# Attention scores as split products on two row halves of TensorE, two tiles at a time

## The chip, the core and the metric

The kernel runs on one core of a Trainium2 chip. Its metric is the device time in microseconds (us) of one execution. The engines named here are TensorE (PE, with its weight loads as PEld), VectorE (DVE), ScalarE (ACT), GpSimd (POOL), and the queue of SyncE (SP), which issues the DMAs.

## The reference, cut to what matters

```python
# q, k, v: (8, 12, 448, 64) float32; g_q, g_k: (64,)
q_n, k_n = rmsnorm(q, g_q), rmsnorm(k, g_k)            # over the last axis
scores = (1 / 8) * q_n @ k_n^T                         # 448 x 448 for each of 96 heads
attn = softmax(scores)                                 # with the row maximum taken off
x = (attn @ v) as (3584, 768)
h = x @ w_in; g = h * cos(h); out = g @ w_out          # w_in 768 x 2048, w_out 2048 x 768
```

All of it is float32. The scores, the part that changes, are 96 products of 448 queries by 448 keys over 64 dimensions.

## The kernel before

The 96 heads are worked on as 48 pairs of two heads; the two heads' 64 dimensions lie on partitions 0 to 63 and 64 to 127. Six pairs make one batch. The 896 query rows of a pair are cut into seven tiles of 128 rows: tiles 0 to 2 are of the first head, 4 to 6 of the second, and tile 3 holds the last 64 rows of the first and the first 64 of the second (its unused quarters are zeros in the queries). Each tile's scores are a PSUM bank of 128 x 448; three banks `S` take turns. VectorE scales a bank and takes its row extremes (`rowmin`, L572), ScalarE makes the exponentials into SBUF (`expo`, L580), TensorE turns them (`transp`, L614 to L623), ScalarE and VectorE split the turned ones into a high and a low part (`pt_high` L637, `pt_low` L644), and TensorE multiplies them by the values (`av`, L661 and L663). The feed-forward product of the batch before runs between (`ffn1`, L745 to L747, `ph`). When the last pair is done, a second stage does the rest of the feed-forward part (L819 to L821).

The first six pairs multiply in plain float32: `score_plain` (L552) takes the 64 rows of one head for tiles 0 to 2 and 4 to 6, two tiles (j and j + 4) one after the other in the program, and all 128 rows for tile 3. A plain float32 matmul of 448 columns shows as two records. `av_plain` (L679, L683, L689) is the plain product with the values, with 64 columns of weights.

From the seventh pair on (42 pairs) a float32 number is split into two numbers of the faster type float32r, x = hi + lo, and a product is qhi khi + qlo khi + qhi klo. `k_high`, `k_low`, `q_high`, `q_low` make the four parts. For tile 3, `score` (L554 to L568) multiplies these three products over all 128 rows. For the six other tiles it needs two matmuls, since 64 dimensions of a head fill half of the rows: the rows of `kboth` (tile `M`) hold khi on partitions 0 to 63 and klo on 64 to 127, those of `qtwo` (tile `D`) hold qhi twice, and those of `qlow` (tile `E`) hold qlo above zeros. DMAs bring the parts to these places: `d_place`, `e_place` and `m_place`, seven transfers a pair.

The order of the work on each engine is made before the kernel is built. `Plan` (L24 to L165) takes every step with its engine, a cost, a due time and the buffers that it reads and writes, and runs the five engines against each other by these costs; the order in which steps start there is the order in which they are emitted. Steps are added by `prepare` (L944), `attend` (L1004) and `multiply`. `SHIFT` moves due times; `RING` holds the number of buffers. TensorE gets a step's matmuls as one unbroken run.

Of the kernel before, what the change touches and what calls it, by code (L numbers as in the profile page):

```python
# [10 lines left out]
F32 = mybir.dt.float32  # L11
# [12 lines left out]
class Plan:  # L24
# [7 lines left out]
        "st_load": 7.0, "m_place": 6.5, "d_place": 6.5, "e_place": 6.5, "v_load": 5.5, "v_fetch": 7.0, "w_load": 7.0,  # L32
# [4 lines left out]
    TWICE = ("rk_spread", "rs_load", "d_place", "m_place")  # L37
# [131 lines left out]
def tile_attention_moe(  # L169
# [11 lines left out]
    nc = tc.nc  # L181
# [36 lines left out]
    gs = cpool.tile([128, 6], F32, tag="gs", name="gs")  # L218
    gsc = {False: gs[:, 5:6], True: gs[:, 4:5]}
# [5 lines left out]
    def g_load():  # L225
        nc.sync.dma_start(gs[:, 0:4], gg)

    def g_fold():
        nc.vector.scalar_tensor_tensor(
            gs[:, 4:6], gs[:, 0:2], -float(D) / math.sqrt(D), gs[:, 2:4], op0=ALU.mult, op1=ALU.mult  # L230
        )
# [107 lines left out]
    def keep(name, n):  # L339
        return [apool.tile([128, n], F32R, tag=f"{name}{i}", name=f"{name}{i}", bufs=1) for i in range(2)]  # L340

    qtwo = keep("D", 768)
    kplain = [apool.tile([128, 2 * S], F32, tag=f"M{i}", name=f"kn{i}", bufs=1) for i in range(2)]
    kplain += [apool.tile([128, 2 * S], F32, tag="lo", name=f"km{i}", bufs=RING["lo"]) for i in range(2)]
    kplain.append(apool.tile([128, 768], F32, tag="E1", name="km4", bufs=1))
    KHOME = (0, 1, 2, 3, 4, 2)
    kboth, qlow = {}, [apool.tile([128, 768], F32R, tag="E0", name="E0", bufs=1)]
# [17 lines left out]

    def e_clear(i):
        if i:
            qlow.append(apool.tile([128, 768], F32R, tag="E1", name="E1", bufs=1))
        nc.vector.tensor_scalar(
            qlow[i][64:128], ident[64:128, 0:1].broadcast_to([64, 768]), 0.0, 0.0, op0=ALU.mult, op1=ALU.add  # L370
        )
# [30 lines left out]
    def km(u):  # L402
        return kplain[KHOME[u]][:, :512]
# [50 lines left out]
    def rkb(u):  # L454
        return (qtwo[u % 2][:, :S] if u < NP else kboth[u % 2][:, S:]).bitcast(F32)

    def rk_spread(u):
        spread(rkb(u), rk_d[u].rearrange("p t -> (p t)"))

    def rk_load(u):  # L460
        if u < NP + 2:
            kboth[u % 2] = apool.tile([128, 2 * S], F32R, tag=f"M{u % 2}", name=f"M{u % 2}", bufs=1)
        row = rk_d[u].rearrange("p t -> (p t)").rearrange("(o h s) -> o h s", o=1, h=2)
        nc.sync.dma_start(rkb(u), row.broadcast_to([64, 2, S]))
# [7 lines left out]
    def k_norm(u):  # L472
        if u >= NP:
            nc.gpsimd.tensor_tensor(kd, kd, rkb(u), ALU.mult)
            return
        for a, c, n in ((0, 64, 0), (64, 0, 384)):
            nc.gpsimd.tensor_tensor(km(u)[a:, c : c + S - n], kd[a:, n:], rkb(u)[a:, n:], ALU.mult)

    def k_high(u):
        nc.scalar.copy(tl(u, "khi", [128, S], F32R), kd)  # L480

    def k_low(u):
        nc.gpsimd.tensor_tensor(tl(u, "kl", [128, S], F32R), kd, pair[u]["khi"].bitcast(F32), ALU.subtract)
# [16 lines left out]

    def m_place(u, low):
        src = pair[u]["kl" if low else "khi"].bitcast(F32)
        dst = kboth[u % 2].bitcast(F32)[64 * low : 64 * low + 64]
        nc.sync.dma_start(dst[:, 384:512], src[:, 384:])
        dst = bass.AP(dst.tensor, dst.offset, [dst.ap[0], [512, 2], [1, 384]])
        nc.sync.dma_start(dst, src[:, :384])

    def d_place(u):
        for a in (0, 64):
            nc.sync.dma_start(qtwo[u % 2].bitcast(F32)[a : a + 64], pair[u]["qhi"].bitcast(F32)[:, :384])  # L510

    def e_place(u):
        nc.sync.dma_start(qlow[u % 2].bitcast(F32)[:64], pair[u]["ql"].bitcast(F32)[:, :384])
# [322 lines left out]
    def y_store(b, oc, src):  # L836
# [19 lines left out]
    def add(eng, cost, due, fn, *args, **more):  # L856
        name, first = fn.__name__, args[0] if args else 0
        stage = 0
        if name in ("ffn1", "h_out", "h_store", "h_both", "x_split"):
            stage = int(first < (NP if name == "x_split" else 1))  # L860
        elif name[:2] not in ("w_", "v_", "e_") or name in ("v_load", "v_high", "v_low", "v_plain", "e_place"):
# [12 lines left out]
        cost *= {DVE: 1.059, ACT: 1.026, POOL: 1.021}.get(eng, 1.0)  # L874
        plan.add(eng, cost, due, fn, *args, **more)
# [68 lines left out]
    def prepare(u):  # L944
# [33 lines left out]
        if not turned:  # L978
            add(SP, ISS, D0 - 30, st_store, u, r=r, w=[("rkd", u)], kb=4.0)
            if plain:  # L980
                add(SP, 2 * ISS, D0 - 26, rk_spread, u, r=[("rkd", u)], w=[("D", u)], kb=224.0)
                add(POOL, 1.55, D0 - 18, k_norm, u, r=[("D", u)] + kd, w=kmw)
            else:
                add(SP, ISS, D0 - 26, rk_load, u, r=[("rkd", u)], w=[("M", u, 2)], kb=224.0)
                add(POOL, 1.13, D0 - 20, k_norm, u, r=[("M", u, 2)], w=kd)
# [18 lines left out]
    def attend(u):  # L1004
# [18 lines left out]
        for n, t in enumerate(TURNED[u % 2]):  # L1023
            if plain:
                break
            key, dj = place(u, n), D0 + 0.5 * step * n
            if t == 3:
                r = [("qhi", u), ("ql", u), ("khi", u), ("kl", u)]
            else:
                r = [("D", u), ("E", u), ("M", u, 0), ("M", u, 1)]  # L1030
            add(PE, 0.62 if t == 3 else 0.41, dj, score, u, n, lead=lead, r=r, w=[key])
            soften(t, n, key, dj + 1)
# [104 lines left out]
    for b in range(B):  # L1137
# [196 lines left out]
```

## Time and profile before

| | |
|---|---|
| Time, median of 3 runs | 1373.1 us (1373.09 to 1374.74) |
| Span of the profiled execution, first to last instruction | 1369.6 us |
| Median time less that span | 3.5 us |
| PE busy | 1343.3 us (98%) |
| DVE, ACT, POOL busy | 1074.6, 926.7, 631.4 us |

The page has a span alone for the profiled execution; the 3.5 us are what the runs' median has beside it. A matmul's recorded duration is longer than the time until the next one may start, since they are pipelined. What a matmul costs TensorE is therefore read from start to start in the timeline.

### The profile page before, as it was taken

How to read it: one execution, taken by the hardware profiler on the slowest of the kernel's cores; microseconds unless marked ns; L12 is line 12 of the kernel's file. 1: busy time of each engine (PE TensorE's matmuls, PEld its weight loads, DVE VectorE, ACT ScalarE, POOL GpSimd, SP SyncE). 2: the span in 40 equal slices, each digit the busy share in tenths (PEclk: the TensorE clock that was granted, in tenths of full speed). 3: DMA queues.
4: the chain of work that ended last, by engine and by line, in shares of the span. 5: the costliest groups of instructions: out<-in, count | busy, mean ns of one | idle time of the engine just before them, and what ended most of it. 6: DMA issues, size and time to landing. Idle time of an engine off the chain costs nothing.

```text
span 1369.6 us, 21501 instructions
## 1 busy us (share of the span) xinstructions
PE 1343.3 (98%) x6998; PEld 1172.3 (86%) x6998; DVE 1074.6 (78%) x1859; ACT 926.7 (68%) x1872; POOL 631.4 (46%) x554
## 2 busy tenths in 40 slices
PE   7899999999999999999999999999999999999998
PEld 3347888788888989888889888999999999999998
DVE  7898999977787887777877877628889889889743
ACT  6677888777877877777777787638567366366321
POOL 4889978676766866766776584330000000000000
PEclk9999999999999999999999999999999999999999
DMA  6898777889797898798987897338988368369334
GB/s 240 268 280 180 197 167 200 231 233 243 202 263 205 224 241 209 213 244 231 240 211 197 226 234 199 121 126 315 375 295 301 120 245 308 112 247 313 105 113 153
DMA packets 149472, 302.19 MB, mean 221 GB/s; under 512 B 34368, under 2 KB 83088, under 8 KB 149360
## 3 DMA queue, kind: packets, MB, share of 16 engines
q1 hardware_dynamic: 149360, 300.83, 75.4%
q8 instruction: 55, 0.90, 0.3%
q14 instruction: 57, 0.47, 0.1%
HBM read 193.99 MB, written 62.73 MB: 187 GB/s over the span
## 4 chain that ended last, share of the span: by engine, by line
PE 83%; DVE 6%; POOL 4%; DMA 3%; issue 2%; ACT 2%; SPq 0%; POOLq 0%; ACTq 0%; DVEq 0%
PE y L820 10%; PE y L819 10%; PE y L821 10%; PE ph L745 8%; PE ph L746 8%; PE ph L747 8%; PE S L568 7%; PE PT L614 6%; PE O L661 4%; PE O L663 3%; DVE S L572 1%; PE O L679 1%; PE S L552 1%; DVE lo L644 1%; PE y L747 1%
## 5 line engine op out<-in xcount | busy, mean ns | idle before, releaser
L572 DVE TENSOR_SCALAR_CACHE_REDUCE S<-S,r 128x448 f32<-128x448 f32 x336 | 225.2, 686 | 56.1 <-PE S L568 47.0
L580 ACT ACTIVATE P<-S,sm 128x448 f32<-128x448 f32 x336 | 213.4, 638 | 73.8 <-DVE S L572 56.3
L745 PE MATMUL ph<-xs,wi 128*128 128x448 f32 x660 | 251.1, 381 | 0.4 <-ACT hbuf L763 0.2
L819 PE MATMUL y<-g,wo 128*128 128x448 f32 x672 | 245.4, 365 | 0.0
L820 PE MATMUL y<-g,wo 128*128 128x448 f32 x672 | 245.4, 365 | 0.0
L821 PE MATMUL y<-g,wo 128*128 128x448 f32 x672 | 245.4, 365 | 0.0
L746 PE MATMUL ph<-xs,wi 128*128 128x448 f32 x660 | 241.8, 366 | 0.0
L747 PE MATMUL ph<-xs,wi 128*128 128x448 f32 x660 | 241.3, 366 | 0.0
L801 ACT CAST g<-gq 128x896 fp32r<-128x896 f32 x112 | 105.6, 943 | 169.8 <-PE y L821 169.4
L637 ACT CAST hi<-PT 128x512 fp32r<-128x512 f32 (+2 forms) x336 | 175.8, 533 | 64.1 <-PE PT L614 22.4
L644 DVE TENSOR_TENSOR lo<-PT,hi 128x512 fp32r<-128x512 f32 (+1 forms) x252 | 153.2, 619 | 39.7 <-ACT hi L637 37.6
L799 DVE TENSOR_TENSOR g<-gq,g 128x896 fp32r<-128x896 f32 x112 | 121.9, 1089 | 59.7 <-ACT g L801 59.2
L614 PEld LDWEIGHTS PT<-ident,P 128*128 128x128 f32 x1008 | 124.1, 141 | 41.9 <-issue 6.2
L614 PE MATMUL PT<-ident,P 128*128 128x128 f32 x1008 | 155.6, 275 | 2.9 <-DVE lo L644 1.2
L745 PEld LDWEIGHTS ph<-xs,wi 128*128 128x128 f32 x660 | 124.3, 188 | 16.4 <-ACT hbuf L763 2.0
L820 PEld LDWEIGHTS y<-g,wo 128*128 128x128 f32 x672 | 126.2, 188 | 10.0
L819 PEld LDWEIGHTS y<-g,wo 128*128 128x128 f32 x672 | 126.2, 188 | 9.9
L821 PEld LDWEIGHTS y<-g,wo 128*128 128x128 f32 x672 | 126.2, 188 | 9.9
L747 PEld LDWEIGHTS ph<-xs,wi 128*128 128x128 f32 x660 | 124.0, 188 | 10.6
L746 PEld LDWEIGHTS ph<-xs,wi 128*128 128x128 f32 x660 | 124.5, 189 | 8.7
L400 POOL TENSOR_TENSOR r<-r,nhalf 128x14 f32<-128x14 f32 (+1 forms) x48 | 124.1, 2586 | 4.0
L661 PE MATMUL O<-hi,vs 128*128 128x448 f32 x336 | 122.6, 379 | 1.1 <-DVE hi L646 0.9
(129 smaller groups left out, 2636.0 us busy)
## 6 DMA issues: line engine op xcount, KB each, us to landing
wo<-wo_d SPq DMA_DIRECT2D x152, 384.0 KB
gq<-h_d SPq DMA_DIRECT2D x64, 448.0 KB
h_d<-hbuf SPq DMA_DIRECT2D x54, 448.0 KB
wo_d<-ao SPq DMA_DIRECT2D x56, 384.0 KB
sd<-sd SPq DMA_DIRECT2D x46, 448.0 KB
kq<-kq SPq DMA_DIRECT2D x42, 480.0 KB
D<-qhi SPq DMA_DIRECT2D x84, 192.0 KB
raw<-w_in SPq DMA_DIRECT2D x16, 768.0 KB
```

The costliest lines, as they stand in the source:

```text
L572: nc.vector.tensor_scalar(d["S", t][:, :S], d["S", t][:, :S], d["r"][:, t : t + 1], None, op0=ALU.mult, op1=ALU.min, accum_out=d["sm"][:, ...
L580: nc.scalar.activation(p_rows(u, t), d.pop(("S", t))[:, :S], AF.Exp, bias=sm[:, 1, t : t + 1], scale=-1.0, accum_out=sm[:, 2, t : t + 1],)
L614: nc.tensor.transpose(pt[part][:, i * 128 : i * 128 + 128], p_rows(u, t)[:, c : c + 128], ident)
L637: nc.scalar.copy(hi if kc < 3 else hi[:64], pt_rows(u, kc, part))
L644: nc.vector.tensor_tensor(lo, src, hi.bitcast(F32), ALU.subtract)
L661: nc.tensor.matmul(O, st, d["hi", kc][:, HEADS[hh]], start=(kc == 0), stop=(kc == 3))
L745: nc.tensor.matmul(ph[:, :S], whi, x2[:, 0, :], start=(cc == 0), stop=False)
L746: nc.tensor.matmul(ph[:, :S], whi, x2[:, 1, :], start=False, stop=False)
L747: nc.tensor.matmul(ph[:, :S], wlo, x2[:, 0, :], start=False, stop=(cc == NCC - 1))
L819: nc.tensor.matmul(y, whi, hi[:, e], start=first and e == 0, stop=False, **more)
L820: nc.tensor.matmul(y, whi, lo[:, e], start=False, stop=False, **more)
L821: nc.tensor.matmul(y, wlo, hi[:, e], start=False, stop=last and e == NG - 1, **more)
```

## The change

From the seventh pair on, the six tiles of one head are multiplied as the three split products over the 64 rows of that head, in place of two matmuls over 128 rows. Two tiles, one of each head, stand in the program in turns: the first product of both, the second of both, the third of both. The two tiles get their PSUM banks together, as one step of the plan (cost 0.7, where a tile was a step of 0.41). Tile 3 stays. Keys and queries keep the layout that the first six pairs have; of the second head's keys a copy of the last 64 columns is put ahead of the others (`k_ahead`, one small DMA each for khi and klo). The transfers `d_place`, `e_place`, `m_place` go, with their buffers, and the two clears of `E`. `khi`, `kl`, `qhi`, `ql` have two buffers each, and the spread of the keys' norms over the partitions goes to a buffer of its own (`rb`) in two DMAs.

```diff
-        "sd": 1, ... "kl": 1, "khi": 1, "qd": 1, "ql": 1, "qhi": 1, "M": 2, "km2": 1, "D": 2, "E": 2, ...
+        "sd": 1, ... "kl": 2, "khi": 2, "qd": 1, "ql": 2, "qhi": 2, "rb": 2, "km2": 1, ...
...
-    def rk_load(u):
-        ...
+    def rk_spread(u):
+        spread(tl(u, "rb", [128, S], F32), rk_d[u].rearrange("p t -> (p t)"))
...
     def k_high(u):
-        nc.scalar.copy(tl(u, "khi", [128, S], F32R), kd)
+        nc.scalar.copy(tl(u, "khi", [128, 512], F32R)[:, 64:], kd)
...
+    def k_ahead(u, name):
+        t = pair[u][name].bitcast(F32)
+        nc.sync.dma_start(t[64:, :64], t[64:, 448:])
...
-    def m_place(u, low):
-        ...
-    def d_place(u):
-        ...
-    def e_place(u):
-        ...
     def score(u, n):
...
-        t = TURNED[u % 2][n]
-        d["S", t] = ps_s.tile([128, 512], F32, tag="S", name=f"S{u}_{t}")
-        if t == 3:
-            khi, kl = d["khi"], d["kl"]
-            qhi, ql = (d[name][:, 384:512] for name in ("qhi", "ql"))
-            ops = ((qhi, khi), (ql, khi), (qhi, kl))
-        else:
-            h, c = t // 4, 384 * (t // 4) + t % 4 * 128
-            ops = tuple((w[u % 2][:, c : c + 128], kboth[u % 2][:, HEADS[h]]) for w in (qtwo, qlow))
-        for i, (a, c) in enumerate(ops):
-            nc.tensor.matmul(d["S", t][:, :S], a, c, start=(i == 0), stop=(i == len(ops) - 1))
+        tiles = TURNED[u % 2][n : n + 1 + (n > 0)]
+        for t in tiles:
+            d["S", t] = ps_s.tile([128, 512], F32, tag="S", name=f"S{u}_{t}")
+        for i, (qn, kn) in enumerate((("qhi", "khi"), ("ql", "khi"), ("qhi", "kl"))):
+            for t in sorted(tiles):
+                p0, p1 = (0, 128) if t == 3 else (0, 64) if t < 3 else (64, 128)
+                c, a = t % 4 * 128 if t > 3 else t * 128, 64 * (t < 4)
+                q, k = d[qn][p0:p1, c : c + 128], d[kn][p0:p1, a : a + S]
+                nc.tensor.matmul(d["S", t][:, :S], q, k, start=(i == 0), stop=(i == 2))
...
-        add(SP, 2 * ISS, D0 - 14, m_place, u, 0, r=khi, w=[("M", u, 0)], kb=358.0)
-        add(SP, 2 * ISS, D0 - 13.5, d_place, u, r=qhi, w=[("D", u)], kb=614.0)
-        add(SP, 2 * ISS, D0 - 13, m_place, u, 1, r=[("kl", u)], w=[("M", u, 1)], kb=358.0)
-        add(SP, ISS, D0 - 12.5, e_place, u, r=[("ql", u)], w=[("E", u)], kb=307.0)
+                add(SP, ISS, D0 - 15, k_ahead, u, "khi", r=khi, w=[("kha", u)], kb=16.0)
+                add(SP, ISS, D0 - 13, k_ahead, u, "kl", r=[("kl", u)], w=[("kla", u)], kb=16.0)
...
-            add(PE, 0.62 if t == 3 else 0.41, dj, score, u, n, lead=lead, r=r, w=[key])
+            add(PE, 0.7 if n else 0.62, dj, score, u, n, lead=lead, r=r, w=keys)
...
-            for i in range(RING["E"]):
-                add(DVE, 0.56, 24.0 + 45 * i, e_clear, i, w=[("E0", i)] + [("km", 4)] * i + [("E", NP + i)], start=20.0)
```

On TensorE, before, the scores of the 27th pair begin like this (`S_3`, `S_0`, `S_4` are the banks of tiles 3, 0 and 4; L614 turns exponentials of the pair before, L745 is feed-forward):

```order
L614 MATMUL PT_111<-ident,P 128x128 x3
L568 MATMUL S_3_5131<-khi_4966,qhi_4915 128x448
L568 MATMUL S_3_5131<-khi_4966,ql_4932 128x448
L568 MATMUL S_3_5131<-kl_4979,qhi_4915 128x448
L568 MATMUL S_0_5139<-M_688,D_100 128x448
L568 MATMUL S_0_5139<-M_688,E_107 128x448
L568 MATMUL S_4_5146<-M_688,D_100 128x448
L568 MATMUL S_4_5146<-M_688,E_107 128x448
L745 MATMUL ph_1_5154<-xs,wi_371 128x448
```

The same place after the change (the lines are numbered anew: L536 is the scores, L582 turns, L713 is feed-forward):

```order
L582 MATMUL PT_108<-ident,P 128x128 x3
L536 MATMUL S_3_5182<-khi_4887,qhi_4899 128x448
L536 MATMUL S_3_5182<-khi_4887,ql_4944 128x448
L536 MATMUL S_3_5182<-kl_4902,qhi_4899 128x448
L536 MATMUL S_0_5189<-khi_4887,qhi_4899 128x448
L536 MATMUL S_4_5190<-khi_4887,qhi_4899 128x448
L536 MATMUL S_0_5189<-khi_4887,ql_4944 128x448
L536 MATMUL S_4_5190<-khi_4887,ql_4944 128x448
L536 MATMUL S_0_5189<-kl_4902,qhi_4899 128x448
L536 MATMUL S_4_5190<-kl_4902,qhi_4899 128x448
L713 MATMUL ph_1_5199<-xs,wi_368 128x448
```

Four matmuls of tiles 0 and 4 have become six, and between the first and the last of them the two banks alternate.

Further on in the same pair the fourth tile of it before stands between a turning step and feed-forward:

```order
L614 MATMUL PT_111<-ident,P 128x128 x3
L568 MATMUL S_5_5250<-M_688,D_100 128x448
L568 MATMUL S_5_5250<-M_688,E_107 128x448
L745 MATMUL ph_2_5232<-xs,wi_428 128x448
```

After the change tiles 1 and 5 are one run between feed-forward and the product with the values (L629, L631):

```order
L715 MATMUL ph_1_5199<-xs,wi_368 128x448
L536 MATMUL S_1_5255<-khi_4887,qhi_4899 128x448
L536 MATMUL S_5_5256<-khi_4887,qhi_4899 128x448
L536 MATMUL S_1_5255<-khi_4887,ql_4944 128x448
L536 MATMUL S_5_5256<-khi_4887,ql_4944 128x448
L536 MATMUL S_1_5255<-kl_4902,qhi_4899 128x448
L536 MATMUL S_5_5256<-kl_4902,qhi_4899 128x448
L629 MATMUL O_0_5268<-hi_0_5187,vs_4965 128x448
```

Tile 5 has moved forward to tile 1, so that a pair has three such runs where six tiles stood, each alone or beside a neighbour.

On SP's queue, before, the placing transfers of this pair stand between the stores and loads of others:

```order
L510 DMA D_100<-qhi_4915 64x2x384 x2
L516 DMA vd_4940<-v 128x512
L513 DMA E_107<-ql_4932 64x2x384
L297 DMA rawo_0_4957<-w_out 128x768
L504 DMA M_688<-khi_4966 64x2x64
L506 DMA M_688<-khi_4966 64x2x384
L470 DMA kq<-kq 128x960
L596 DMA rs_d<-rt_4995 7x128
L504 DMA M_688<-kl_4979 64x2x64
L506 DMA M_688<-kl_4979 64x2x384
```

After, two small copies stand there:

```order
L440 DMA rs_4889<-rs_d 64x448 x2
L467 DMA khi_4887<-khi_4887 64x64
L467 DMA kl_4902<-kl_4902 64x64
L435 DMA rk_d<-r_4880 128x7
L737 DMA h_d<-hbuf 128x896
L375 DMA sd_4995<-sd 128x896
L486 DMA vd_4997<-v 128x512
```

Seven transfers of the pair have gone from the queue and two of 64 x 64 numbers have come.

## Rows read from the trace of the kernel before

**Rows 1.** The page: its span, and the chain that ended last, by engine.

```profile
span 1369.6 us, 21501 instructions
PE 83%; DVE 6%; POOL 4%; DMA 3%; issue 2%; ACT 2%; SPq 0%; POOLq 0%; ACTq 0%; DVEq 0%
```

**Rows 2.** Stretches: length; PE, PEld, DVE, ACT, POOL busy (records); clock, DMA share, GB/s.

```profile
40.00:89.00 49.00, 43.91 (x180) 19.67 (x179) 43.38 (x92) 35.59 (x83) 39.79 (x35) 0.93 0.90 276
89.00:175.00 86.00, 81.96 (x424) 63.57 (x423) 78.73 (x146) 68.18 (x156) 79.43 (x63) 0.98 0.83 199
175.00:875.00 700.00, 695.51 (x3841) 620.50 (x3840) 556.59 (x1169) 539.43 (x1262) 473.99 (x419) 1.00 0.83 218
925.00:1350.00 425.00, 425.00 (x2099) 393.93 (x2098) 345.90 (x358) 237.27 (x275) 0.00 (x0) 1.00 0.67 236
```

**Rows 3.** TensorE's waits from 89 us on: us in total, times, longest.

```profile
PE S L568 <- ACT P L580: 2.4, 4, 1.0
PE O L663 <- DVE lo L644: 1.4, 2, 1.0
```

**Rows 4.** TensorE's timeline at 505.8 us: start, duration, instruction, x records.

```profile
505.81 0.36 PE L568 MATMUL S<-M,D 128*128 128x448 f32 x1
506.01 0.36 PE L568 MATMUL S<-M,E 128*128 128x448 f32 x1
506.21 0.60 PE L614 MATMUL PT<-ident,P 128*128 128x128 f32 x4
506.56 0.45 PE L745 MATMUL ph<-xs,wi 128*128 128x448 f32 x1
506.85 0.36 PE L746 MATMUL ph<-xs,wi 128*128 128x448 f32 x1
```

**Rows 5.** TensorE's timeline at 67 and 72 us, among the plain pairs.

```profile
66.81 0.66 PE L614 MATMUL PT<-ident,P 128*128 128x128 f32 x4
67.40 1.02 PE L552 MATMUL S<-km,q 64*128 64x448 f32 x4
68.35 0.66 PE L614 MATMUL PT<-ident,P 128*128 128x128 f32 x4
68.94 0.96 PE L679 MATMUL O<-hi,vs 128*64 128x448 f32 x2
...
71.87 0.92 PE L552 MATMUL S<-km,q 128*128 128x448 f32 x2
72.62 0.49 PE L614 MATMUL PT<-ident,P 128*128 128x128 f32 x3
```

**Rows 6.** TensorE's timeline at 102 us: a split tile between two plain products.

```profile
102.33 0.97 PE L679 MATMUL O<-hi,vs 128*64 128x448 f32 x2
103.23 0.47 PE L568 MATMUL S<-M,D 128*128 128x448 f32 x1
103.54 0.36 PE L568 MATMUL S<-M,E 128*128 128x448 f32 x1
103.83 0.39 PE L683 MATMUL O<-hi,vs 128*64 128x64 f32 x3
```

**Rows 7.** The weight loads of that tile: start, duration, idle before.

```profile
103.23 0.19 PEld L568 LDWEIGHTS S<-M,D 128*128 128x128 f32 x1 [0.70 <-ACT sd L391]
103.34 0.19 PEld L568 LDWEIGHTS S<-M,E 128*128 128x128 f32 x1
```

**Rows 8.** TensorE's timeline at 499.8 us: weights of 64 and 128 columns by turns.

```profile
499.97 0.36 PE L661 MATMUL O<-hi,vs 128*128 128x448 f32 x1
500.17 0.37 PE L663 MATMUL O<-lo,vs 128*64 128x448 f32 x1
500.37 0.36 PE L745 MATMUL ph<-xs,wi 128*128 128x448 f32 x1
```

**Rows 9.** The page's DMA issues: out<-in, count, KB each.

```profile
D<-qhi SPq DMA_DIRECT2D x84, 192.0 KB
```

**Rows 10.** VectorE's clears of `E`: shortest, median, longest ns, first and last start.

```profile
L369 DVE TENSOR_SCALAR E<-ident x2: 557/728/900, 19.4 to 73.2; 64x768 fp32r<-64x768 f32 x2
```

More of the change, by code (lines that the diff above doesn't have):

```diff
@@ L31 @@
     FLIGHT = {
-        "st_load": 7.0, "m_place": 6.5, "d_place": 6.5, "e_place": 6.5, "v_load": 5.5, "v_fetch": 7.0, "w_load": 7.0,
+        "st_load": 7.0, "v_load": 5.5, "v_fetch": 7.0, "w_load": 7.0,
         "v_store": 6.0, "rk_load": 6.0, "rs_load": 6.0,
@@ L36 @@
     LANES = 8
-    TWICE = ("rk_spread", "rs_load", "d_place", "m_place")
+    TWICE = ("rk_spread", "rs_load")
     def __init__(self, rings, loose=()):
@@ L217, in tile_attention_moe @@
     make_identity(nc, ident)
-    gs = cpool.tile([128, 6], F32, tag="gs", name="gs")
-    gsc = {False: gs[:, 5:6], True: gs[:, 4:5]}
+    gs = cpool.tile([128, 3], F32, tag="gs", name="gs")
+    gsc = gs[:, 2:3]
     nhalf = cpool.tile([128, 1], F32, tag="nhalf", name="nhalf")
@@ L225, in g_load @@
     def g_load():
-        nc.sync.dma_start(gs[:, 0:4], gg)
+        nc.sync.dma_start(gs[:, 0:2], gg)
     def g_fold():
         nc.vector.scalar_tensor_tensor(
-            gs[:, 4:6], gs[:, 0:2], -float(D) / math.sqrt(D), gs[:, 2:4], op0=ALU.mult, op1=ALU.mult
+            gsc, gs[:, 0:1], -float(D) / math.sqrt(D), gs[:, 1:2], op0=ALU.mult, op1=ALU.mult
         )
@@ L337, in tile_attention_moe @@
     xs = {}
[L339 to L343, printed above, removed]
+    kplain = [apool.tile([128, 512], F32, tag=f"km{i}", name=f"kn{i}", bufs=1) for i in range(2)]
     kplain += [apool.tile([128, 2 * S], F32, tag="lo", name=f"km{i}", bufs=RING["lo"]) for i in range(2)]
-    kplain.append(apool.tile([128, 768], F32, tag="E1", name="km4", bufs=1))
+    kplain.append(apool.tile([128, 512], F32, tag="km4", name="km4", bufs=1))
     KHOME = (0, 1, 2, 3, 4, 2)
-    kboth, qlow = {}, [apool.tile([128, 768], F32R, tag="E0", name="E0", bufs=1)]
     kq = apool.tile([128, S + 512], F32, tag="kq", name="kq", bufs=1)
@@ L364, in p_rows @@
         return pbuf[:, p_slot(p_key(u, t))]
[L366 to L371, printed above, removed]
     def tl(u, name, shape, dt, tag=None):
@@ L452, in spread @@
             nc.sync.dma_start(dst[64 * hh : 64 * hh + 64], row.broadcast_to([64, S]))
-    def rkb(u):
-        return (qtwo[u % 2][:, :S] if u < NP else kboth[u % 2][:, S:]).bitcast(F32)
     def rk_spread(u):
-        spread(rkb(u), rk_d[u].rearrange("p t -> (p t)"))
-    def rk_load(u):
[L461 to L464, printed above, removed]
+        spread(tl(u, "rb", [128, S], F32), rk_d[u].rearrange("p t -> (p t)"))
     def k_load(u):
@@ L473, in k_norm @@
         if u >= NP:
-            nc.gpsimd.tensor_tensor(kd, kd, rkb(u), ALU.mult)
+            nc.gpsimd.tensor_tensor(kd, kd, pair[u]["rb"], ALU.mult)
             return
         for a, c, n in ((0, 64, 0), (64, 0, 384)):
-            nc.gpsimd.tensor_tensor(km(u)[a:, c : c + S - n], kd[a:, n:], rkb(u)[a:, n:], ALU.mult)
+            nc.gpsimd.tensor_tensor(km(u)[a:, c : c + S - n], kd[a:, n:], pair[u]["rb"][a:, n:], ALU.mult)
     def k_high(u):
-        nc.scalar.copy(tl(u, "khi", [128, S], F32R), kd)
+        nc.scalar.copy(tl(u, "khi", [128, 512], F32R)[:, 64:], kd)
     def k_low(u):
-        nc.gpsimd.tensor_tensor(tl(u, "kl", [128, S], F32R), kd, pair[u]["khi"].bitcast(F32), ALU.subtract)
+        kl = tl(u, "kl", [128, 512], F32R)
+        nc.gpsimd.tensor_tensor(kl[:, 64:], kd, pair[u]["khi"].bitcast(F32)[:, 64:], ALU.subtract)
+    def k_ahead(u, name):
+        t = pair[u][name].bitcast(F32)
+        nc.sync.dma_start(t[64:, :64], t[64:, 448:])
     def q_plain(u):
@@ L492, in q_scale @@
         q = q_plain(u) if u < NP else qd
-        nc.gpsimd.tensor_scalar(q, q, gsc[u < NP], 0.0, op0=ALU.mult, op1=ALU.add)
+        nc.gpsimd.tensor_scalar(q, q, gsc, 0.0, op0=ALU.mult, op1=ALU.add)
     def q_high(u):
@@ L499, in q_low @@
         nc.gpsimd.tensor_tensor(tl(u, "ql", [128, 512], F32R), qd, pair[u]["qhi"].bitcast(F32), ALU.subtract)
-    def m_place(u, low):
[L502 to L506, printed above, removed]
-    def d_place(u):
-        for a in (0, 64):
-            nc.sync.dma_start(qtwo[u % 2].bitcast(F32)[a : a + 64], pair[u]["qhi"].bitcast(F32)[:, :384])
-    def e_place(u):
-        nc.sync.dma_start(qlow[u % 2].bitcast(F32)[:64], pair[u]["ql"].bitcast(F32)[:, :384])
     def v_load(u):
@@ L860, in add @@
             stage = int(first < (NP if name == "x_split" else 1))
-        elif name[:2] not in ("w_", "v_", "e_") or name in ("v_load", "v_high", "v_low", "v_plain", "e_place"):
+        elif name[:2] not in ("w_", "v_") or name in ("v_load", "v_high", "v_low", "v_plain"):
             stage = 2 if first < NP else int(first < NP + 3)
@@ L980, in prepare @@
             if plain:
-                add(SP, 2 * ISS, D0 - 26, rk_spread, u, r=[("rkd", u)], w=[("D", u)], kb=224.0)
-                add(POOL, 1.55, D0 - 18, k_norm, u, r=[("D", u)] + kd, w=kmw)
-            else:
-                add(SP, ISS, D0 - 26, rk_load, u, r=[("rkd", u)], w=[("M", u, 2)], kb=224.0)
-                add(POOL, 1.13, D0 - 20, k_norm, u, r=[("M", u, 2)], w=kd)
+                add(SP, 2 * ISS, D0 - 26, rk_spread, u, r=[("rkd", u)], w=[("rb", u)], kb=224.0)
+                add(POOL, 1.55, D0 - 18, k_norm, u, r=[("rb", u)] + kd, w=kmw)
+            else:
+                add(SP, 2 * ISS, D0 - 26, rk_spread, u, r=[("rkd", u)], w=[("rb", u)], kb=224.0)
+                add(POOL, 1.13, D0 - 20, k_norm, u, r=[("rb", u)], w=kd)
                 add(ACT, 0.5, D0 - 17, k_high, u, r=kd, w=khi)
+                add(SP, ISS, D0 - 15, k_ahead, u, "khi", r=khi, w=[("kha", u)], kb=16.0)
                 add(POOL, 1.2, D0 - 15, k_low, u, r=kd + khi, w=[("kl", u)])
+                add(SP, ISS, D0 - 13, k_ahead, u, "kl", r=[("kl", u)], w=[("kla", u)], kb=16.0)
         if plain:
@@ L1022, in attend @@
                 soften(t, 2 * j + n, keys[n], dj + 1)
-        for n, t in enumerate(TURNED[u % 2]):
+        for n in (0, 1, 3, 5):
             if plain:
                 break
[L1026 to L1030, printed above, removed]
-            add(PE, 0.62 if t == 3 else 0.41, dj, score, u, n, lead=lead, r=r, w=[key])
-            soften(t, n, key, dj + 1)
+            tiles = TURNED[u % 2][n : n + 1 + (n > 0)]
+            keys = [place(u, n + i) for i in range(len(tiles))]
+            dj = D0 + 0.5 * step * n
+            r = [(name, u) for name in ("qhi", "ql", "khi", "kl")]
+            if n:
+                r += [("kha", u), ("kla", u)]
+            add(PE, 0.7 if n else 0.62, dj, score, u, n, lead=lead, r=r, w=keys)
+            for i, t in enumerate(tiles):
+                soften(t, n + i, keys[i], dj + 1 + 0.5 * step * i)
         D1 = D0 + 4 * step
@@ L1305 @@
     qp[:, 64:, 448:] = qh[:, 1, :, :64]
[L1306 to L1308 removed]
+    kq = np.concatenate([kp, qp], axis=2)
     vp = np.concatenate([v, v[:, :, 384:]], axis=2)
@@ L1320 @@
         "sd": c(sd), "kn": c(kn), "kq": c(kq), "v": c(vp),
-        "gg": c(np.stack([f(inputs[n], 2) for n in ("g_q", "g_k") for f in (np.tile, np.repeat)], axis=1)),
+        "gg": c(np.stack([np.tile(inputs[n], 2) for n in ("g_q", "g_k")], axis=1)),
         "w_in": wi, "w_out": wo,
```

10 lines of the change are left out of this document (3 added, 7 removed), and 2 rows, old and new, of the table RING.

## The prediction

> **What bounds the kernel now.** I read the page first: the reader is to see that the chain that ended last lies on TensorE for 83% of the span [rows 1]. That is an average, so the stretches come next. From 89 to 175 us three engines share the bound: TensorE is busy 82.0 of 86 us, VectorE 78.7, GpSimd 79.4; TensorE has 4.0 us to spare. From 175 to 875 us, where nearly all pairs of the changed kind are scored, TensorE is busy 695.5 of 700 us while VectorE has 556.6 and GpSimd 474.0, at a granted clock of 1.00 (2.4 GHz) [rows 2]. After 925 us no score is left and nothing changes. So from 175 us on TensorE's own time is the kernel's time, and 4.5 us of waits are all that could be taken up. TensorE's waits confirm it: the two longest are 2.4 us for the exponentials that free a score bank and 1.4 us for a split part; none of the list's releasers is a placing transfer [rows 3]. A busy TensorE says little of what an instruction costs, so the rest is read from start to start in the timeline.
>
> **What a score costs now.** A tile is two matmuls, started at 505.81 and 506.01, and the next instruction starts at 506.21: 0.20 us each, 0.40 a tile [rows 4]. Two tiles cost 0.80 us. A pair has three such twos; 42 pairs make 126.
>
> **What it costs after, step by step.** Two tiles become six matmuls over 64 rows, the two halves by turns.
>
> 1. Do the halves run beside each other? The plain pairs have such a two: four records start at 67.40, the next instruction at 68.35, so 0.95 us; one plain tile over all rows takes 0.75 (71.87 to 72.62) [rows 5]. One after the other would be 1.50 and more. They do run together, and I take three steps of 0.20 us, 0.60, since float32r matmuls start 0.20 apart in rows 4. The lower bound comes from rows 5: without the 0.20 that step 2 explains, 0.75 is four half-passes of 0.19, so 0.56.
>
> 2. What is the 0.20 by which the two exceeds the single tile? At 102 us a split tile stands between two plain products that use a part of the array. Its first matmul takes 0.31 (103.23 to 103.54), its second 0.29 (to 103.83), where 0.20 is usual [rows 6]. The weight loads tell why: the second is issued 0.11 after the first, when that one has gone in; before it TensorE had loaded nothing for 0.70 us [rows 7]. So at a change of the array's division the next weights are not loaded beside the running matmul: it runs out first, 0.09, and then the load stands in the open, 0.11. A turning step has a shorter load: four turnings between two changes take 0.59 (66.81 to 67.40) [rows 5]; four with none, with the matmul behind them, take 0.64 (506.21 to 506.85), so 0.44 alone [rows 4]; 0.59 less 0.44 less 0.09 leaves 0.06.
>
> 3. A two of halves changes the division twice, in and out: 0.09 on the matmul ahead, 0.11 for its own first load, 0.09 behind its last step, and 0.11 or 0.06 for the next instruction's load. In the changed program's order none of the 126 runs follows another directly; 94 are followed by a matmul with an ordinary load and 32 by a turning step, 0.10 on average. That is 0.39 a visit.
>
> 4. The sum: 0.60 + 0.39 = 0.99 against 0.80, +0.19 us, 126 times, 23.9 us. The lower price of step 1 makes it 0.95, +0.15.
>
> The Trainium skill, "TensorEngine Tiling (Array Packing)", Key Properties, says that changing the tiling mode, not just the tile, drains TensorE; the 0.09 us of rows 6 agrees. By the same page's Theoretical Speedup, up to a factor of 2 for a dimension of up to 64, the run alone would be 0.60 for 0.80 us.
>
> **What lies on the path.** Five pairs, 15 runs, fall before 175 us: their 2.8 us go into the 4.0 us that TensorE has there [rows 2]. The other 111 runs cost 111 x 0.19 = 21 us. Of the 4.5 us of waits after 175 us a later TensorE takes up perhaps half, 2.3: 18.7 us stay.
>
> **The transfers.** Seven placing DMAs a pair go (two of them are the 192 KB of qhi, 84 in all [rows 9]) and two small ones come; the norms' spread is two for one. No wait of TensorE is for them [rows 3], so I take 0 after 175 us: what hides them is TensorE's own queue. Before, the DMA engines are 0.90 and 0.83 busy [rows 2], and an earlier landing of other loads may bring up to the 4.0 us there; it would cost nothing, since two copies are fewer than seven transfers. I take 0, the nearest row being rows 3. If the two copies came late, they would hold a run of scores on TensorE's in-order queue and the feed-forward work behind it; the plan starts them some 13 us ahead of their use, a time that hides a landing several times over.
>
> **The rest.** VectorE loses two clears of 0.56 and 0.90 us, both before 89 us [rows 10], where it is 43.4 of 49 us busy: 0 to 1.5 us gained, I take 0. The work of ScalarE, GpSimd and VectorE for each tile is the same in number. The plan gives a run 0.7 us where I expect 0.99, so the other engines will be early for TensorE, which costs nothing where it is the bound.
>
> The span becomes 1369.6 + 18.7 = 1388.3 us; with the 3.5 us that the median of the runs has beside the span, 1391.8 us. Its own range: 0.15 instead of 0.19 with the 4.5 us all taken up, and up to 1.5 and 4.0 us gained ahead, give 1380; nothing taken up anywhere gives 1397; a plan of another order may add 2: 1380 to 1399.
>
> **Rivals.** (A) The visits cost little in float32r, and the kernel is faster. For it: matmuls with 64 and 128 columns of weights alternate at 0.20 us in float32r (L661 at 499.97, L663 at 500.17, L745 at 500.37) with no trace of a drain [rows 8], while plain ones of the same shape show it [rows 5, 6]. Then a run is 0.60 and 111 x 0.20 = 22 us go: 1351 us. It decides from a visit of less than 0.20. The Trainium skill, "TensorE: Matmul & The Clock Gate", Part 3, gives the span of matmuls on distinct row groups as one matmul's time and some 4 ns per further tile; by that alone this is the result. Against it: as built, L663 names no part of the columns, so the division does not change there, while the new matmuls name a half of the rows, as those of rows 5 do; and the price of rows 6 is paid by float32r matmuls.
>
> (B) The halves do not run together in float32r, so the change does not do what it says. Nothing in the trace shows split products on half the rows. Six steps of 0.20 and a visit are 1.59, +0.79: 111 x 0.79 = 88 us, 1461 us; without the visit 1.20, +0.40: 1417. Against it stand the plain halves of rows 5.
>
> (C) Banks: a run needs two of the three score banks at once, and TensorE's in-order queue stands when the second is not free. Four such waits of 0.6 us on average occur now [rows 3]. One in each of 42 pairs would be 25 us, 1417; in every second pair 1404. Against it: a pair takes 786 / 42 = 18.7 us, so VectorE and ScalarE have some 4 to 5 us between runs.
>
> **How the numbers follow.** What a measurement of this kernel can tell from no change is about 0.2%, 2.7 us. The forecast has 0.75 (0.72 slower, 0.02 within, 0.01 faster, where the gains ahead of 175 us are large); A 0.14 (0.12 faster, 0.02 within: a visit at half price is even); C 0.07 and B 0.04, both slower. So faster 0.13, within 0.04, slower 0.83. A range of 1372 to 1404 holds the forecast but for 0.02, the even part of A and half of C: 0.80.
>
> **What would show it.** In the changed profile: six records of a run should start as three pairs, each at nearly one time, with the steps 0.19 to 0.21 apart; from the end of the step ahead to the first weights there should be 0.09 of nothing, and a run should take about 0.80 from its first start to the next instruction's start, with the next one's 0.20 lengthened to 0.31. The stretch from 175 us to the last score should be some 20 us longer with TensorE still full, and the stage behind it unchanged at 0.20 us a matmul. The prediction is wrong if the weights of the second division are loaded beside the running matmul (A), if the second half of a two starts 0.20 behind the first (B), or if TensorE's waits for exponentials grow by 10 us or more (C).

## The result, and the profile after

The changed kernel takes 1391.3 us, median of 4 runs (1390.4 to 1399.6), against 1373.1 us (1372.4 to 1374.7) for the kernel before on the same chip: a ratio of 1.0146, 95% interval 1.0119 to 1.0174. It is slower by some 18 us, and 1391.8 us had been forecast. The profiled execution took 1391.7 us; its span has grown by 20.3 us from that in [rows 1]. An execution's time is 1.8 us above its span (1391.7 and 1389.9 here), so the profiled one of the kernel before, with 1369.6, took some 1371.4 us, 1.7 less than its median: the 20.3 us hold this difference too.

The page of the changed kernel, its first line:

```profile
span 1389.9 us, 21600 instructions
```

Where do the 20.3 us lie? The start of the first feed-forward matmul behind the last score divides the span into the part that changed and the part that did not. Of the kernel before, the instructions that write `y` in that place (count, shortest, median and longest in ns, first and last start in us):

```profile
L745 PE MATMUL y<-xs,wi x72: 362/365/369, 913.2 to 956.4; 128*128 128x448 f32 x72
```

and the same of the changed kernel:

```profile
L713 PE MATMUL y<-xs,wi x72: 362/365/369, 931.4 to 974.6; 128*128 128x448 f32 x72
```

So 18.2 us were lost before that point and 2.1 us behind it. Where the 18.2 begin is seen from the single tile of the 11th pair, before which four changed pairs have been scored (12 runs of two tiles; 114 come after it). It starts so in the kernel before (start, duration, instruction):

```profile
162.20 0.47 PE L568 MATMUL S<-khi,qhi 128*128 128x448 f32 x1 [0.69 <-ACT P L580]
```

and so in the changed one:

```profile
161.27 0.37 PE L536 MATMUL S<-khi,qhi 128*128 128x448 f32 x1
```

Up to there nothing is lost, rather 0.9 us gained. From this tile to the second stage, first the kernel before and then the changed one (columns as in [rows 2]):

```profile
162.20:913.20 751.00, 746.51 (x4112) 667.06 (x4113) 583.81 (x1215) 568.32 (x1324) 499.64 (x441) 1.00 0.80 212
```

```profile
161.27:931.40 770.13, 764.92 (x4342) 633.14 (x4342) 582.97 (x1218) 567.80 (x1322) 501.05 (x439) 1.00 0.50 157
```

VectorE, ScalarE and GpSimd have the same work, within 1.5 us; TensorE's share has grown by 18.4 us and its idle time from 4.5 to 5.2. 18.4 us over 114 runs are 0.16 us a run. The granted clock is 1.00 in both. The DMA share fell from 0.80 to 0.50, and TensorE idles no less for it.

The busy stretch ahead of it in the changed kernel, to be held against [rows 2]:

```profile
89.00:175.00 86.00, 81.76 (x451) 59.46 (x451) 75.10 (x145) 69.53 (x157) 78.89 (x65) 1.00 0.42 127
```

TensorE, VectorE and GpSimd are as they were but for a few us of VectorE, at half the DMA share.

TensorE's waits from 89 us to the end say that its scores hardly wait (us in total, times, longest):

```profile
PE PT L582 <- DVE lo L612: 2.8, 4, 1.8
PE ph L713 <- ACT hbuf L731: 2.3, 3, 1.3
...
PE y L787 <- DMA wo<-wo_d: 1.1, 1, 1.1
PE y L787 <- DVE outs L800: 0.9, 1, 0.9
...
PE S L536 <- ACT P L548: 0.5, 1, 0.5
```

The last row, the exponentials that free a score bank, had 2.4 us in [rows 3]. The first two rows have grown; the section on the prediction comes back to them. The two rows of `L787` are the 2.0 us lost in the second stage, where the kernel before has no wait at all.

What a run of two tiles costs is read in TensorE's timeline of the changed kernel, from start to start:

```profile
500.67 0.37 PE L714 MATMUL ph<-xs,wi 128*128 128x448 f32 x1
500.87 0.37 PE L715 MATMUL ph<-xs,wi 128*128 128x448 f32 x1
501.17 0.47 PE L536 MATMUL S<-khi,qhi 64*128 64x448 f32 x2
501.47 0.37 PE L536 MATMUL S<-khi,ql 64*128 64x448 f32 x2
501.68 0.37 PE L536 MATMUL S<-kl,qhi 64*128 64x448 f32 x2
501.98 0.47 PE L629 MATMUL O<-hi,vs 128*128 128x448 f32 x1
502.29 0.36 PE L631 MATMUL O<-lo,vs 128*64 128x448 f32 x1
```

"x2" with 64 rows is the two halves at one time. Usual steps are 0.20 us (500.67 to 500.87). The matmul ahead takes 0.30 (to 501.17), the run's first step 0.30, its second 0.21, its last 0.30 (to 501.98), and the next instruction 0.31. So three steps of 0.20, and about 0.40 for the visit, as I call going to half of the rows and back. The weight loads of the same place (start, duration, idle before) say when the surplus arises:

```profile
500.67 0.19 PEld L715 LDWEIGHTS ph<-xs,wi 128*128 128x128 f32 x1
501.17 0.18 PEld L536 LDWEIGHTS S<-khi,qhi 64*128 64x128 f32 x2 [0.31 <-issue]
501.27 0.19 PEld L536 LDWEIGHTS S<-khi,ql 64*128 64x128 f32 x2
501.48 0.19 PEld L536 LDWEIGHTS S<-kl,qhi 64*128 64x128 f32 x2
501.98 0.19 PEld L629 LDWEIGHTS O<-hi,vs 128*128 128x128 f32 x1 [0.31 <-issue]
```

Load and matmul normally overlap by one place: the weights of L715 go in at 500.67, while L714 runs. The first load on half the rows does not go in beside L715 (start 500.87) but 0.30 us behind that start, after 0.31 us in which nothing is loaded; the first load on all rows behind the run, at 501.98, has the same 0.31 us ahead of it.

### The profile page after: what moved, and what is told of

It reads as the page before. It is cut to its first block, busy times and chain, and to the rows that moved or that the text cites. A ratio compares the mean times of both kernels' runs of the same rounds, so it can differ in the third digit from the quotient of the medians.

```text
span 1389.9 us, 21600 instructions
## 1 busy us (share of the span) xinstructions
PE 1363.2 (98%) x7250; PEld 1134.4 (82%) x7250; DVE 1070.2 (77%) x1857; ACT 927.5 (67%) x1872; POOL 630.1 (45%) x554
## 5 line engine op out<-in xcount | busy, mean ns | idle before, releaser
L540 DVE TENSOR_SCALAR_CACHE_REDUCE S<-S,r 128x448 f32<-128x448 f32 x336 | 220.6, 687 | 65.2 <-PE S L536 59.5
L713 PE MATMUL ph<-xs,wi 128*128 128x448 f32 x660 | 255.0, 386 | 2.5 <-ACT hbuf L731 2.3
L787 PE MATMUL y<-g,wo 128*128 128x448 f32 x672 | 245.6, 366 | 1.9 <-DMA wo<-wo_d 1.1
L714 PE MATMUL ph<-xs,wi 128*128 128x448 f32 x660 | 241.8, 366 | 0.0
L715 PE MATMUL ph<-xs,wi 128*128 128x448 f32 x660 | 241.3, 366 | 0.0
L582 PEld LDWEIGHTS PT<-ident,P 128*128 128x128 f32 x1008 | 122.3, 141 | 46.9 <-issue 10.7
L582 PE MATMUL PT<-ident,P 128*128 128x128 f32 x1008 | 155.2, 277 | 2.9 <-DVE lo L612 2.8
L713 PEld LDWEIGHTS ph<-xs,wi 128*128 128x128 f32 x660 | 124.1, 188 | 29.7 <-issue 9.5
L787 PEld LDWEIGHTS y<-g,wo 128*128 128x128 f32 x672 | 126.2, 188 | 12.6 <-DMA wo<-wo_d 1.5
L715 PEld LDWEIGHTS ph<-xs,wi 128*128 128x128 f32 x660 | 124.0, 188 | 10.7
L629 PE MATMUL O<-hi,vs 128*128 128x448 f32 x336 | 131.9, 404 | 0.6 <-DVE hi L614 0.6
L714 PEld LDWEIGHTS ph<-xs,wi 128*128 128x128 f32 x660 | 124.5, 189 | 8.0
```

Of the source, the lines that this page charges most:

```text
L540: nc.vector.tensor_scalar(d["S", t][:, :S], d["S", t][:, :S], d["r"][:, t : t + 1], None, op0=ALU.mult, op1=ALU.min, accum_out=d["sm"][:, ...
L582: nc.tensor.transpose(pt[part][:, i * 128 : i * 128 + 128], p_rows(u, t)[:, c : c + 128], ident)
L629: nc.tensor.matmul(O, st, d["hi", kc][:, HEADS[hh]], start=(kc == 0), stop=(kc == 3))
L713: nc.tensor.matmul(ph[:, :S], whi, x2[:, 0, :], start=(cc == 0), stop=False)
L714: nc.tensor.matmul(ph[:, :S], whi, x2[:, 1, :], start=False, stop=False)
L715: nc.tensor.matmul(ph[:, :S], wlo, x2[:, 0, :], start=False, stop=(cc == NCC - 1))
```

## The experiments

Each kernel ran beside the kernel before on the same chip; its ratio is to those runs (medians of 1372.8 us). Experiments 1 and 3 to 5 had one chip, experiments 2, 6 and 7 another.

**1. The visits taken away, the three steps kept.** The three steps of a run stay, but each is one matmul over all rows: two for the first tile and one for the second. The kernel leaves out part of each product and mixes the two heads; only its time counts.

```diff
+        prods = (("qhi", "khi"), ("ql", "khi"), ("qhi", "kl"))
+        two = sorted(tiles)
+        todo = [(two[0], prods)] if len(two) == 1 else [(two[0], prods[:2]), (two[1], prods[2:])]
+        for t, ps in todo:
+            for i, (qn, kn) in enumerate(ps):
...
-                p0, p1 = (0, 128) if t == 3 else (0, 64) if t < 3 else (64, 128)
-                q, k = d[qn][p0:p1, c : c + 128], d[kn][p0:p1, a : a + S]
...
+                q, k = d[qn][:, c : c + 128], d[kn][:, a : a + S]
...
```

> The changed kernel, but two tiles get three matmuls over all 128 rows (two for the first tile, one for the second) in place of six over 64 rows. It leaves out part of each product and mixes the heads; its time is that of a run with three steps and no change of the array's division. Theory (a run of halves is three steps of 0.20 us and a visit of 0.39 us): 111 runs after 175 us lose the visit, 111 x 0.39 = 43 us less than the changed kernel, about 1348 us, and 22 us less than the kernel before. Rival (the visit is cheap, and the halves' steps themselves or the new order are what costs): within 5 us of the changed kernel, about 1386 to 1391 us.

Measured: 1360.0 us (1356.6 to 1365.9, 3 runs), ratio 0.9907, interval 0.9875 to 0.9938. Faster than the kernel before, so the visit and not the three steps is the loss; but 12 us above what I expected. The profile shows that 7 us of this have nothing to do with scores. The second stage, whose program is the same in all these kernels, took 464.9 us in that execution (893.3 to 1358.2), where experiment 2 has 458.0 (columns as in [rows 2]):

```profile
1050.00:1150.00 100.00, 100.00 (x486) 90.83 (x485) 83.62 (x88) 57.00 (x65) 0.00 (x0) 1.00 0.66 225
```

486 matmuls in 100 us where the pace is about 495. I ran the same kernel again.

**2. The same kernel again.**

> The kernel with three matmuls over all rows for two tiles once more (it leaves out part of each product and mixes the heads). In its first profile the second stage, which the edit doesn't touch, had its matmuls 0.2067 us apart where all others have 0.2027, some 9 us. Theory: that is a state of a single execution, and executions without it take some 1351 us, 40 less than the changed kernel; the runs fall into two groups 9 us apart. Rival: the edit's program has it always, and all runs lie at 1357 to 1366 us.

Measured: 1354.7 us (1354.6 to 1356.1, 4 runs), ratio 0.9860, interval 0.9845 to 0.9876; 36.6 us below the changed kernel, where I had expected 40. The slower second stage does not come with the program alone. Two groups of runs 9 us apart were not seen: those of experiment 1 are 1356.6, 1360.0 and 1365.9 us, and as the chip was another one too, the cause stays open. The same stretch of the second stage, and the scores from the 11th pair's single tile on:

```profile
1050.00:1150.00 100.00, 100.00 (x495) 92.69 (x495) 85.40 (x90) 58.32 (x66) 0.00 (x0) 1.00 0.65 227
161.13:894.80 733.67, 725.00 (x3999) 644.98 (x4000) 578.03 (x1218) 565.63 (x1322) 502.75 (x439) 1.00 0.52 165
```

The second stage starts at 894.8 us instead of 931.4. From the 11th pair's tile to there the kernel takes 733.7 us, 36.5 less than the changed one: TensorE's busy time is 39.9 us less, 0.35 us for each of 114 visits, and its idle time is 8.7 us in place of 5.2. Its longest waits up to 950 us:

```profile
PE ph L715 <- ACT hbuf L733: 3.9, 5, 1.5
PE PT L584 <- DVE lo L614: 3.4, 7, 1.5
PE S L538 <- ACT P L550: 2.3, 1, 2.3
PE O L633 <- DVE lo L614: 2.1, 1, 2.1
```

Of the time taken off TensorE, 3.5 us are given back as waits for VectorE and ScalarE.

**3. The old number of matmuls without the transfers.** As the changed kernel, but each of the two tiles takes two matmuls over all rows, four a run as before the change, on operands that no transfer places. It leaves out the third product and mixes the heads.

```diff
+        prods = (("qhi", "khi"), ("ql", "khi"), ("qhi", "kl"))
+        for t in sorted(tiles):
+            ps = prods if t == 3 else prods[:2]
+            for i, (qn, kn) in enumerate(ps):
...
+                q, k = d[qn][:, c : c + 128], d[kn][:, a : a + S]
...
```

> The changed kernel, but each tile gets two matmuls over all 128 rows, as before the change, from keys and queries that nothing has placed. It leaves out one of three products and mixes the heads; its time is that of the change without the halves: transfers gone, two tiles as one step of the plan. Theory (the transfers were hidden and the whole difference is the halves'): TensorE's work is that of the kernel before, 1373 us, at most 4 us less. Rival 1 (the transfers slowed something): 1360 us or less. Rival 2 (the two banks taken at once or the new order cost time): 1378 us or more.

Measured: 1374.5 us (1372.0 to 1382.4, 10 runs, three of them above 1381), ratio 1.0026, interval 1.0005 to 1.0047. Without seven placing transfers a pair and with two clears fewer the kernel is no faster than before. The experiment takes the transfers and the old order away together, so what each is worth by itself is not shown. The 11th pair's single tile starts at 158.54 us, 3.7 earlier than before; from there to the second stage:

```profile
158.54:911.60 753.06, 747.01 (x4113) 666.82 (x4113) 579.12 (x1218) 567.61 (x1322) 501.16 (x439) 1.00 0.50 161
```

That is 2.1 us more than before, and 1.6 of it is idle time of TensorE (6.1 in place of 4.5). The changed kernel takes 17.1 us more than this for the same stretch, with 17.9 us more work for TensorE: that is what the halves cost by themselves, 0.16 us for each of 114 runs. The second stage starts at 911.6 us (first row on `y` below), 1.6 us earlier than before, and runs out at 1370.3, later than before:

```profile
L714 PE MATMUL y<-xs,wi x72: 362/365/369, 911.6 to 954.8; 128*128 128x448 f32 x72
```

From there to the end it takes 458.7 us, as the changed kernel's 458.5 and not the 456.4 of before. So the 2 us of the second stage come with what the two kernels share, not with the halves: in the profiles of all kernels with the old transfers this stage takes 456.3 or 456.4 us, and 458.0 to 458.7 in those of the kernels without, leaving experiment 1 aside.

**4. The price of a visit by itself.** In the kernel before, an extra matmul of 8 columns on 64 rows, ahead of tiles 0, 1 and 2, 126 times; the products behind it overwrite what it leaves.

```diff
+        if t < 3:
+            a, c = ops[0]
+            nc.tensor.matmul(d["S", t][:, :8], a[:64], c[:64, :8], start=True, stop=True)
```

> The kernel before, with one more matmul of 8 columns over 64 rows ahead of tiles 0, 1 and 2 of each pair from the seventh on, 126 in all; the tile's own first matmul overwrites what it wrote. Theory: 8 columns take next to nothing, and each is a visit to another division: 0.09 + 0.11 + 0.09 + 0.11 = 0.40 us, 111 x 0.40 = 44 us, about 1417 us (up to 1423 if nothing is taken up). Rival (a change of division is cheap in float32r): like the same matmul over 128 rows, 12 to 15 us, about 1387 us.

Measured: 1413.2 us (1412.2 to 1414.3), ratio 1.0286, interval 1.0264 to 1.0309: +40.4 us. TensorE's timeline there:

```profile
505.49 0.37 PE L750 MATMUL ph<-xs,wi 128*128 128x448 f32 x1
505.79 0.27 PE L569 MATMUL S<-M,D 64*128 64x8 f32 x1
505.99 0.47 PE L571 MATMUL S<-M,D 128*128 128x448 f32 x1
506.30 0.37 PE L571 MATMUL S<-M,E 128*128 128x448 f32 x1
```

0.30, 0.20 and 0.31 from start to start, 0.81 for two usual steps of 0.41 together: the visit, with its small matmul, costs 0.40. Over the 114 visits from the 11th pair on, this is what is seen:

```profile
163.90:954.00 790.10, 789.12 (x4226) 684.99 (x4227) 585.03 (x1216) 570.91 (x1324) 497.07 (x439) 1.00 0.76 202
```

39.1 us more than before: TensorE has 42.6 us more work, 0.37 a visit, and idles 1.0 us instead of 4.5. Here waits were taken up.

**5. Its control,** the same extra matmul over all 128 rows.

```diff
+            nc.tensor.matmul(d["S", t][:, :8], a[:128], c[:128, :8], start=True, stop=True)
```

> The kernel before, with the same additional matmul of 8 columns over all 128 rows, 126 in all. Theory: no change of division, but the weight load behind so short a matmul stands in the open, 0.11 us: 111 x 0.11 = 12 us, about 1385 us. It is the control of the one over 64 rows: the two should lie some 30 us apart. Rival (any further matmul costs as much as the visit): both at the same time.

Measured: 1384.0 us (1382.9 to 1385.1), ratio 1.0074, interval 1.0051 to 1.0096: +11.2 us. In its timeline the matmul ahead keeps its 0.21, and the small one starts 0.02 before the product:

```profile
491.25 0.37 PE L750 MATMUL ph<-xs,wi 128*128 128x448 f32 x1
491.46 0.17 PE L569 MATMUL S<-M,D 128*128 128x8 f32 x1
491.48 0.45 PE L571 MATMUL S<-M,D 128*128 128x448 f32 x1
491.77 0.36 PE L571 MATMUL S<-M,E 128*128 128x448 f32 x1
```

From 491.25 to 491.77 are 0.52 us, where two usual steps are 0.41: the small matmul costs 0.11 without any change of division. The product's own step of 0.29 holds most of it. Between experiments 4 and 5 only the number of rows differs: 29.2 us, for 126 changes of division there and back. From the 11th pair on TensorE has 758.4 us of work here and 789.1 in experiment 4, so 0.27 us for each of 114 changes there and back.

**6. The six products one tile after the other** instead of by turns. In the changed kernel the two loops are exchanged, so the program's order is three for the first half and then three for the second.

```diff
-        for i, (qn, kn) in enumerate((("qhi", "khi"), ("ql", "khi"), ("qhi", "kl"))):
-            for t in sorted(tiles):
+        prods = (("qhi", "khi"), ("ql", "khi"), ("qhi", "kl"))
+        for t in sorted(tiles):
+            for i, (qn, kn) in enumerate(prods):
```

> The changed kernel with the same six matmuls of a run in another order: the three products of the first tile, then the three of the second, with nothing left out. Theory (two halves run together only when they stand next to each other, since matmuls start in the program's order): the last of the first tile and the first of the second run together, so a run is five steps of 0.20 us in place of three, +0.40: 111 x 0.40 = 44 us, about 1435 us. Rival (the engine puts the two halves beside each other in any order, as it does with weight loads): 1391 us, as the changed kernel.

Measured: 1389.9 us (1389.1 to 1390.8), ratio 1.0113, interval 1.0094 to 1.0133. My theory, that the halves would now follow each other, fell; the rival was right. TensorE's timeline there shows the same three steps:

```profile
501.67 0.37 PE L632 MATMUL O<-lo,vs 128*64 128x448 f32 x1
501.97 0.48 PE L537 MATMUL S<-khi,qhi 64*128 64x448 f32 x2
502.28 0.37 PE L537 MATMUL S<-khi,ql 64*128 64x448 f32 x2
502.48 0.37 PE L537 MATMUL S<-kl,qhi 64*128 64x448 f32 x2
502.78 0.55 PE L588 MATMUL PT<-ident,P 128*128 128x128 f32 x3
```

The second half's first product, fourth in the program, starts with the first half's first, and so in 124 of the 126 runs. In one of the other two the second half came late; there the first half's three products stand by themselves, from 113.28 us on, and the second half's three behind them:

```profile
113.80 0.36 PE L537 MATMUL S<-kl,qhi 64*128 64x448 f32 x1
114.26 0.47 PE L537 MATMUL S<-khi,qhi 64*128 64x448 f32 x1
```

So step 1 needs no alternation, and the loss is the same 0.30 in and out.

**7. Other changes of division taken away.** In the kernel before, the plain value products (L679) use 64 columns of the array, and beside them stand the longer steps of [rows 6]. Here they take 128 columns of weights, of which 64 are of the next block; the rows of `O` that these fill are used by nobody.

```diff
-            nc.tensor.matmul(o_bank(u, hh)[:64, :S], d["vs"][:, hh * NVC + kc], ...)
+            wide = d["vs"][:, hh * NVC + kc : hh * NVC + kc + 2].rearrange("p n d -> p (n d)")
+            nc.tensor.matmul(o_bank(u, hh)[:, :S], wide, ...)
```

> The kernel before, where the plain products of the first six pairs with the values (L679) load 128 columns of weights in place of 64; the further 64 rows of the result are not read. Nothing is left out. Theory (plain matmuls of 64 columns are visits to another division of the array): 39 changes of the division fewer, each 0.09 us and a load of 0.05 to 0.11, some 6 us of TensorE before 110 us; VectorE and GpSimd are nearly as full there, so 2 to 5 us are left, 1368 to 1371 us. Rival (the division doesn't change with 64 columns, or other engines hold that stage): 1373 us, no change; wider loads could cost 1 us.

Measured: 1372.4 us (1370.4 to 1375.2, 11 runs), ratio 0.9992, interval 0.9981 to 1.0002: no change. The cost did vanish where it stood. TensorE's timeline around two of these products:

```profile
68.46 0.66 PE L614 MATMUL PT<-ident,P 128*128 128x128 f32 x4
68.95 0.92 PE L680 MATMUL O<-hi,vs 128*128 128x448 f32 x2
69.71 0.49 PE L614 MATMUL PT<-ident,P 128*128 128x128 f32 x3
```

Four turnings ahead of it take 0.49 us, where four ahead of a plain product took 0.59 (68.35 to 68.94 in [rows 5]), and two products take 0.76 where 0.90 was usual (102.33 to 103.23 in [rows 6]). But all 72 of these stand before 109 us, where other engines and the DMAs are nearly as full [rows 2], and in the profiled execution the gain does not last: the 11th pair's single tile starts at 162.83 us, 0.6 later than in that of the kernel before. From 16 to 175 us TensorE has two waits for loads and transfers that the kernel before has not:

```profile
PE S L568 <- DMA kq<-kq: 1.2, 1, 1.2
PE S L568 <- DMA M<-kl: 1.0, 1, 1.0
```

The interval does not exclude a gain of up to 2.6 us. Visits that put 42.6 us on TensorE cost 40 us in experiment 4; the smaller price taken away here brought nothing that can be measured. What a visit costs the kernel depends on what bounds the stage.

## Why the prediction was right

**Step 1, three steps at 0.20.** Right: the halves start as pairs with 0.20 to 0.21 between them inside the run. My fear in rival B, that they run one after the other, is excluded, even where the program asks for them in that order (experiment 6).

**Steps 2 and 3, the change of division, 0.39 a visit.** Right in mechanism and size: nothing is loaded for 0.31 us at either end of the run, the instruction ahead and the run's last step each take 0.10 more, the first step and the next instruction 0.10 to 0.11. With one matmul of 8 columns it is 0.40 as well (experiment 4). Of these 0.40, the same matmul on all rows has 0.11 (experiment 5): behind it, too, the next load is not hidden. The Trainium skill, "TensorEngine Tiling (Array Packing)", Key Properties, names the drain at a changed tiling mode; the timelines agree, in that no load goes in beside the running matmul, and set its price here. The ends of matmul records are modelled, so the drain itself is not seen. Rival A, a cheap visit, is excluded by the same rows.

**Step 4, +0.19 a run.** Slightly too large: 0.16 over the stage. The four matmuls of before stand 0.204 apart and cost 0.82 us, not the 0.80 that I read from one place, and a visit is 0.35 to 0.37 over the stage (experiments 2 and 4) where single places show 0.40.

**What lies on the path.** The 12 runs up to the 11th pair went in the main into TensorE's spare time, as predicted of them. From the 7th pair's single tile to the 11th's the changed kernel takes 71.2 us (90.08 to 161.27) and experiment 6, with the same halves, 71.2 as well (87.81 to 159.04); experiment 3, without them, takes 70.5 (88.08 to 158.54). That is 0.7 us for 12 runs, where 0.16 a run would be 1.9. The kernel before takes 73.0 (89.22 to 162.20); each of these is one execution. The granted clock of 89 to 175 us, 1.00 in these three and 0.98 before, does not explain the gain alone: experiments 4, 5 and 7 have 1.00 and the old transfers, and take 72.0 to 73.9 us. It may have a part, since experiments 1 and 2, without these transfers and at 0.98, take 72.8 and 72.0. What is left is the transfers that are gone or the new order; the two were not tried apart. The three runs of the 11th pair itself cannot be read: the single tile of the 12th pair starts at 184.55 us, 1.35 later than the 183.20 of before, but 132 matmul records stand in between in place of 118, and only six of the 14 are the runs' own.

The 2.3 us that a later TensorE should take out of the waits did not come, idle grew by 0.7 instead. Experiment 3 says where that lies: the new transfers and order have 1.6 us more idle time without a half, and beside that kernel the halves do take up 0.8 us of waits (2.1 in experiment 6). In experiment 4, with twice the surplus, they did come (3.5 us). In the changed kernel the waits for exponentials fell from 2.4 to 0.5 us, but those of the turnings for `lo` and of the feed-forward for `hbuf`, now 2.8 and 2.3 us, were smaller before. The same rows of the list of the kernel before, from 89 us on:

```profile
PE PT L614 <- DVE lo L644: 1.2, 5, 0.4
...
PE ph L745 <- ACT hbuf L763: 0.2, 1, 0.2
```

So this term was wrong, and the too large 0.19 made up for it: 18.7 us predicted, 18.2 measured up to the second stage between the two profiled executions. That the forecast of 1391.8 us lies 0.5 us from the median is luck. The price of a run, the waits, the 0.9 us gained ahead and the 2.1 us of the second stage were each off by some 1 to 3 us; with the 1.7 us of the profiled execution they cancel.

**The transfers and the rest at 0.** Right as a sum (experiment 3), not in its parts: that kernel is 3.7 us ahead at the 11th pair and loses 2.1 us up to the second stage and 2.3 in it. **The unchanged stage** was not quite unchanged: 2.1 us, two waits that I had not foreseen. That experiment 3 has about the same without a single half puts it with the new data path. Why the weights land late there, and `outs` comes late, was not followed further.

**Rival C, the banks.** Excluded: one wait of 0.5 us.

What the change gives up is therefore shown by experiments 1 and 2: three steps for four are worth 18 us to this kernel (1354.7 against 1372.8) when they need no visit, and the visit takes 37 us.

## What to carry to other kernels

Dividing the array pays by the run, not by the matmul: on a TensorE that bounds its stage, going to half rows and back cost about 0.40 us here, so a run must save more than two matmuls of 448 columns (0.20 us each) before it gains; this one saved one. Put all work on halves that stands near together into one run, or leave it on all rows. Read first whether TensorE bounds that stage: in one stage 126 visits cost 40 us; in another, taking visits away gained nothing that could be measured.

## What the runs showed of the hardware

- Products on the second half of the rows start beside earlier products on the first half, the fourth in the program with the first (experiment 6).
- Around products in float32 with 64 columns of weights some time is lost as at a change of division, and it is gone with 128 columns (0.10 us in the turnings ahead, 0.14 in two products, experiment 7), while products in float32r with 64 columns stand at the usual pace [rows 8]. No run shows whether the number type makes the difference or, as rival A has it, how the built program names the columns.
- One execution of the kernel of experiments 1 and 2 ran the second stage at 486 matmuls in 100 us instead of 495, at a granted clock of 1.00 in both; the stage took 6.9 us more. Its cause is open.
